# Cluster attention feeding two FFN stages: the row maxima placed by a small transfer, throwaway products, and a new sequence

## The chip, the cores and the metric

The kernel runs on one core of a Trainium2 chip. TensorE (PE) multiplies, VectorE (DVE), ScalarE (ACT) and GpSimd (POOL) work elementwise, SyncE (SP) issues most transfers. The metric is the device time of one execution in microseconds.

## What is computed

The reference, cut to what matters, with B = 2, H = 8, S = 768, D = 64, 16 clusters, 1536 tokens of 512 numbers, a hidden width of 2048, 8 experts of 4 slots:

```python
q_assign = argmax(normalized(q) @ normalized(centroids).T)   # per head, k the same
mask = q_assign[..., :, None] == k_assign[..., None, :]
scores = where(mask, q @ k.T / sqrt(D), -1e9)
attn = exp(scores - scores.max(-1)); attn /= attn.sum(-1) + 1e-9
x = (attn @ v) laid out as tokens x 512
h = x @ w_in; x = (h * clip(h + 3, 0, 6) / 6) @ w_out
logits = x @ phi                      # soft MoE: d is a softmax over tokens, c over slots
slot_in = d.T @ x; slot_out = relu(slot_in @ w1) @ w2 per expert
out = c @ slot_out
```

## The kernel before

**Heads.** The 16 heads (2 batches of 8) are numbered i. A head has 768 rows in six tiles of 128. Its queries and keys are split into high and low half-precision parts and turned by transposing transfers into two operands: `qk1t` (high and low parts) and `qk2t`, whose partitions 0 to 63 carry the high parts, 64 to 79 the one-hot cluster, and 96 to 101 rows for the maxima. For each tile n, `maxq` (L514) multiplies the first 80 partitions into a tile `sm`, and `maxr` (L530, on DVE) reduces it to one maximum per row, in column 96 + n of `mxs`. When the six columns are there, `shift` turns `mxs` on PE (L537, into a corner of the last `sm` tile) and DVE writes the result, times a diagonal, into the six rows 96 to 101 of `qk2t` (L539). `scores` (L552 with `qk1t`, L556 with 102 partitions of `qk2t`) then gives scores with mask and maximum already subtracted in tile `st`. `exps` (L600, L331 on ACT) makes probabilities, `plow` (L341 on POOL) their low parts, `pv` (L622 to L643) multiplies by v into `acc`, `finish` divides on DVE.

So the first L556 of a head needs the maxima of all six tiles: it waits for L539 of that head.

**FFN.** Every 128 tokens (12 token tiles) `xtrans` turns x by a transfer (L678), `hid` multiplies by w_in (L693), `act` applies the gate (L710, L712, L331, L341), `logits` follows, `dispatch` (L802) adds to `z`. Weights are loaded by SP and split into half-precision parts on DVE and ACT beside the heads (`narrow`, L861 to L871). The FFN of the first batch lies among heads 8 to 15, that of the second behind the last head.

**Tail.** `zsum` and `norm` (L1172, L1177, L1186), `slot_in` (`si`, L1199), `slot_t` (`sit`, L1216), `layer1` (`e`, L1324), `turn` (`ht`, L1348), `layer2` and `layer2_part` (L1361, L1381), `combine` (`po`, L1305) and the stores. Expert weights arrive in `wk` tiles through SP.

**Order.** The kernel is cut into generators (events). A string `ORDER` lists, step by step, which event goes on, and `ROOMS` fixes which buffer each tile takes:

```python
def flush():
    with tc.manual_schedule():
        for x in ORDER.split():
            next(events[int(x)], None)
```

So the order on each engine is what the string says. The queue of SP is one list too: a transfer that waits holds those behind it.

Of the kernel before, what the change touches and what calls it, by code (L numbers as in the profile page):

```python
# [8 lines left out]
F16 = mybir.dt.float16  # L9
# [8 lines left out]
P = 128  # L18
# [202 lines left out]
def clustered_attention_ffn_softmoe(ctx: ExitStack, tc, q, k, v, cent, w_in, w_out, phi, w1, w2, out):  # L221
# [76 lines left out]
    def consts():  # L298
# [6 lines left out]
        for t in qk2:  # L305
            nc.gpsimd.memset(t[:, :, :, 80:128], 0.0)
            nc.gpsimd.memset(t[:, :, 1, 96 : 96 + NT], SH)
            yield

    def consts2():  # L310
# [9 lines left out]
        for t in mxs:  # L320
            nc.gpsimd.memset(t, 0.0)
# [1133 lines left out]
```

## Time and profile before

| what | value |
|---|---|
| median of 3 runs | 486.13 us (485.87 to 487.93) |
| the profiled execution | 487.06 us, of which the span of the core's work is 485.0 us |
| busy share of the span | PE 89%, DVE 60%, ACT 65%, POOL 51% |
| mean granted clock of PE | 0.974 of full speed |

The 2.06 us between the span and the time lie around the work of the engines. The busy shares are means over stages with different limits: heads 0 to 7 with the splitting of weights (to about 135 us), heads 8 to 15 with the FFN of the first batch (to about 328 us), the FFN of the second batch (to about 420 us), and the tail.

### The profile page before, as it was taken

What the parts mean: (1) busy time and instruction counts of PE and PEld (TensorE: products, weight loads), DVE (VectorE), ACT (ScalarE), POOL (GpSimd) and SP (SyncE); (2) the same over time, 40 slices, a digit from 0 to 9 for tenths busy, and PEclk for the clock granted to TensorE, in tenths of its full rate; (3) what the DMA queues carried; (4) which work ended last, traced back from release to release, by engine and by line L of the source; (5) the groups of instructions that cost most, each with busy time, mean ns of one, the idle gap of its engine ahead of it and who ended that gap; (6) DMA issues with size and microseconds to landing.
All of it is one profiled execution on the core that took longest, in us unless ns stands there. A gap on an engine that the chain in (4) does not pass through costs nothing.

```text
span 485.0 us, 11609 instructions
## 1 busy us (share of the span) xinstructions
PE 431.3 (89%) x4802; PEld 275.4 (57%) x4802; DVE 289.4 (60%) x497; ACT 317.6 (65%) x518; POOL 249.3 (51%) x227
## 2 busy tenths in 40 slices
PE   1569899989979999999999998989998999789964
PEld 1337677768767556655656766744544455523443
DVE  4999999999978388466656868313324324421322
ACT  5759899889967679766989998953545444501121
POOL 4337686876545257656869897983133133030000
PEclk9999999999989999999999999999999999789986
DMA  7799767948690985865396533019994999999997
GB/s 226 209 164 203 194 166 202 258 145 226 189 250 18 213 206 109 190 164 106 66 246 148 109 64 66 1 20 189 295 366 95 304 268 330 381 317 351 329 268 223
DMA packets 133813, 95.48 MB, mean 197 GB/s; under 512 B 96385, under 2 KB 119425, under 8 KB 133761
## 3 DMA queue, kind: packets, MB, share of 16 engines
q1 hardware_dynamic: 129088, 88.95, 69.8%
q10 hardware_dynamic: 4672, 5.80, 3.3%
q8 instruction: 37, 0.61, 0.5%
q14 instruction: 16, 0.12, 0.1%
HBM read 64.06 MB, written 7.34 MB: 147 GB/s over the span
## 4 chain that ended last, share of the span: by engine, by line
PE 50%; DVE 17%; DMA 11%; ACT 8%; issue 4%; POOL 4%; SPq 1%; ACTq 0%; DVEq 0%; POOLq 0%
PE h L693 20%; DVE mxs L530 5%; PE sm L514 3%; PE st L552 3%; DMA qk1t<-qk 3%; PE st L556 3%; PE e L1324 3%; DMA wod<-in_moe_w_out_dram 3%; DMA wk<-in_moe_w_dram 2%; DMA qk2t<-qk 2%; ACT p L600 2%; POOL pp L341 2%; PE o L1361 2%; ACT pp L331 1%; PE z L802 1%
## 5 line engine op out<-in xcount | busy, mean ns | idle before, releaser
L341 POOL TENSOR_TENSOR pp<-p,pp 128x768 f16<-128x768 f32 x72 | 117.8, 1645 | 60.1 <-ACT pp L331 34.9
L693 PE MATMUL h<-wq,xt 128*128 128x512 f16 x576 | 131.5, 379 | 1.0 <-DMA xt<-xhl 1.0
L530 DVE TENSOR_REDUCE mxs<-sm 128x1 f32<-128x768 f32 x96 | 88.8, 951 | 15.0 <-PE sm L514 14.4
L693 PEld LDWEIGHTS <-xt 128*128 128x128 f16 x576 | 55.4, 98 | 64.0 <-issue 2.5
L341 POOL TENSOR_TENSOR ghl<-r,ghl 128x1024 f16<-128x1024 f32 (+1 forms) x25 | 50.3, 2011 | 71.3 <-ACT ghl L331 61.3
L600 ACT ACTIVATE p<-st 128x768 f32<-128x768 f32 x72 | 58.0, 809 | 9.2 <-PE st L556 7.5
L331 ACT ACTIVATE pp<-p 128x768 f16<-128x768 f32 x72 | 60.3, 843 | 1.2
L552 PE MATMUL st<-qk1t 128*128 128x384 f16 x192 | 48.2, 333 | 6.0 <-ACT p L600 2.8
L712 DVE SCALAR_TENSOR_TENSOR r<-r,h 128x1024 f32<-128x1024 f32 (+1 forms) x26 | 29.5, 1136 | 36.8 <-ACT r L710 35.4
L514 PE MATMUL sm<-qk2t 80*128 80x384 f16 x192 | 46.0, 338 | 4.1 <-DVE mxs L530 1.9
L556 PE MATMUL st<-qk2t 102*128 102x384 f16 x192 | 48.4, 333 | 0.0
L710 ACT ACTIVATE r<-h,b_relu 128x1024 f32<-128x1024 f32 (+1 forms) x26 | 27.2, 1045 | 30.9 <-PE h L693 19.2
L622 PE MATMUL acc<-v,pp 128*128 128x65 f32 x288 | 36.2, 276 | 0.2 <-DVE oh L457 0.2
L622 PEld LDWEIGHTS acc<-v,pp 128*128 128x128 f32 x288 | 35.2, 194 | 1.7 <-issue 0.5
L628 PE MATMUL acc<-v,pp 128*128 128x64 f16 x432 | 36.1, 194 | 0.0
L627 PE MATMUL acc<-v,pp 128*128 128x65 f16 x432 | 36.1, 192 | 0.0
L341 POOL TENSOR_TENSOR qk<-qk,qk 128x768 f16<-128x768 f32 x15 | 25.5, 1698 | 19.4 <-ACT qk L331 19.1
L331 ACT ACTIVATE ghl<-r 128x1024 f16<-128x1024 f32 (+1 forms) x26 | 25.6, 987 | 13.4 <-DVE r L712 11.1
L627 PEld LDWEIGHTS <-pp 128*128 128x128 f16 x432 | 31.2, 99 | 2.7
L628 PEld LDWEIGHTS <-pp 128*128 128x128 f16 x432 | 29.2, 96 | 2.7
L331 ACT ACTIVATE qk<-qk 128x768 f32<-128x768 f32 (+2 forms) x32 | 25.9, 818 | 6.0 <-DMA qk1t<-qk 4.2
L635 PE MATMUL acc<-v,pp 128*128 128x65 f16 x432 | 24.9, 194 | 2.6 <-POOL pp L341 2.6
(193 smaller groups left out, 763.5 us busy)
## 6 DMA issues: line engine op xcount, KB each, us to landing
wk<-in_moe_w_dram SPq DMA_DIRECT2D x60, 512.0 KB, 8.3
wi<-in_moe_w_in_dram SPq DMA_DIRECT2D x16, 512.0 KB, 6.3
wod<-in_moe_w_out_dram SPq DMA_DIRECT2D x16, 512.0 KB, 4.8
wos<-wo ACTq DMA_DIRECT2D x8, 512.0 KB, 3.6
wk<-wos SPq DMA_DIRECT2D x8, 512.0 KB, 5.0
qk<-in_q_dram SPq DMA_DIRECT2D x16, 192.0 KB, 3.5
qk<-in_k_dram SPq DMA_DIRECT2D x16, 192.0 KB, 3.8
v<-in_v_dram SPq DMA_DIRECT2D x16, 192.0 KB, 2.9
```

The source lines that it names most:

```text
L331: nc.scalar.activation(out, in_, AF.Copy, scale=scale)
L341: (nc.vector if e == "v" else nc.gpsimd).tensor_tensor(out=out, in0=in_, in1=hi, op=ALU.subtract)
L514: nc.tensor.matmul(s[:, j, 0:384], d["qk2t"][0:80, n, 0], d["qk2t"][0:80, 3 * j : 3 * j + 3, 1], start=True, stop=True,)
L530: nc.vector.tensor_reduce(out=mxs[i % 2][:, 96 + n : 97 + n], in_=s[:, :, 0:384], op=ALU.max, axis=AX.XY)
L552: nc.tensor.matmul(s[:, j, 0:384], d["qk1t"][:, t, 1], d["qk1t"][:, 3 * j : 3 * j + 3, 0], start=True, stop=False)
L556: nc.tensor.matmul(s[:, j, 0:384], d["qk2t"][0 : 96 + NT, t, 1], d["qk2t"][0 : 96 + NT, 3 * j : 3 * j + 3, 0], start=False, stop=True,)
L600: nc.scalar.activation(p32, s[:, :, 0:384], AF.Exp, scale=sc_exp)
L622: nc.tensor.matmul(o, p32[:, j, r * P : (r + 1) * P], d["v32"][:, t], start=(t == 0 and n == 0), stop=False)
L627: nc.tensor.matmul(o, hi, v1[:, t, 0:65], start=(t == 0 and n == 0), stop=False)
L628: nc.tensor.matmul(o[:, 0:64], hi, v1[:, t, 65:129], start=False, stop=False)
L693: nc.tensor.matmul(s[:, fb % 2], xt[:, lhs], wq[fb][:, hl, kk], start=(n == 0), stop=(n == 11))
L712: nc.vector.scalar_tensor_tensor(out=g, in0=r, scalar=6.0 * SG, in1=sf, op0=ALU.min, op1=ALU.mult)
```

## The change

The turned maxima become six rows of 128 numbers on six partitions. One DVE operation (L556 of the changed kernel) scales them into a small tile `row`, and a transfer from SP (L558) lays the 768 numbers one behind the other into a single partition (96) of `qk2t`. `mxs` shrinks to six columns, the score product reads 97 partitions in place of 102, and a constant row of the operand is one row in place of six. A function `keep` issues matmuls into a PSUM tile that nobody reads; 47 of these events (108 products) stand ahead of the turn of head 1's maxima, one (two products) among the last heads, and 13 (26 products) in the tail. `ORDER` and `ROOMS` are new.

```diff
-    mxs = [ap.tile([P, 96 + NT], F32, name=f"mxs_{i}", bufs=1) for i in range(2)]
+    mxs = [ap.tile([P, NT], F32, name=f"mxs_{i}", bufs=1) for i in range(2)]
-            nc.gpsimd.memset(t[:, :, 1, 96 : 96 + NT], SH)
+            nc.gpsimd.memset(t[:, :, 1, 96:97], SH)
-        for t in mxs:
-            nc.gpsimd.memset(t, 0.0)
+    def keep(n, m):
+        t = pss(f"kw_{n}")
+        for _ in range(m):
+            nc.tensor.matmul(t[:, 0, 0:256], ident16, ident.bitcast(F16), start=True, stop=True)
+        yield
-            d["mt"] = s[0 : 96 + NT, 0, 384:512]
+            d["mt"] = s[0:NT, 0, 384:512]
-        nc.vector.tensor_reduce(out=mxs[i % 2][:, 96 + n : 97 + n], in_=s[:, :, 0:384], op=ALU.max, axis=AX.XY)
+        nc.vector.tensor_reduce(out=mxs[i % 2][:, n : n + 1], in_=s[:, :, 0:384], op=ALU.max, axis=AX.XY)
         nc.tensor.transpose(pm, mxs[i % 2], ident)
         yield
-        nc.vector.scalar_tensor_tensor(
-            out=d["qk2t"][96 : 96 + NT, :, 0],
-            in0=pm[96 : 96 + NT].unsqueeze(1).to_broadcast([NT, NT, P]),
-            scalar=-(2.0**29),
-            in1=nident[96 : 96 + NT, 96 : 96 + NT].unsqueeze(2).to_broadcast([NT, NT, P]),
-            op0=ALU.max,
-            op1=ALU.mult,
-        )
+        row = sm.tile([NT, P], F16, tag="row", name=f"row_{i}", bufs=2)
+        nc.vector.tensor_scalar(out=row, in0=pm, scalar1=-1.0 / SH, scalar2=2.0**29 / SH, op0=ALU.mult, op1=ALU.min)
+        yield
+        nc.sync.dma_start(out=d["qk2t"][96:97, :, 0], in_=row)
-                d["qk2t"][0 : 96 + NT, t, 1],
-                d["qk2t"][0 : 96 + NT, 3 * j : 3 * j + 3, 0],
+                d["qk2t"][0:97, t, 1],
+                d["qk2t"][0:97, 3 * j : 3 * j + 3, 0],
+    for n in range(7):
+        ev(keep, n, 4)
+    for n in range(40):
+        ev(keep, 7 + n, 2)
+    for n in range(14):
+        ev(keep, 47 + n, 2)
```

Head 8 on DVE, before. The rows are the last reductions of its maxima (`mxs`), the division of head 7 (`den`, `xa`), and the write of the six rows (L539):

```order
L530 TENSOR_REDUCE mxs_113<-sm_3_2346 128x1
L652 TENSOR_SCALAR den_2383<-acc_2231 128x6
L653 RECIPROCAL den_2383<-den_2383 128x6
L655 TENSOR_TENSOR xa_2386<-acc_2231,den_2383 128x384
L530 TENSOR_REDUCE mxs_113<-sm_0_2388 128x1
L440 TENSOR_TENSOR as_2295<-as_2295,ac_2408 128x12x16
L539 SCALAR_TENSOR_TENSOR qk2t_2290<-sm_5_2326,nident 6x6x128
L443 TENSOR_REDUCE mx_2452<-as_2295 128x12
```

The same place on DVE in the changed program:

```order
L546 TENSOR_REDUCE mxs_113<-sm_5_2490 128x1
L546 TENSOR_REDUCE mxs_113<-sm_0_2510 128x1
L664 TENSOR_SCALAR den_2547<-acc_2407 128x6
L665 RECIPROCAL den_2547<-den_2547 128x6
L667 TENSOR_TENSOR xa_2550<-acc_2407,den_2547 128x384
L556 TENSOR_SCALAR row_2569<-sm_5_2490 6x128
L456 TENSOR_TENSOR as_2577<-as_2577,ac_2608 128x12x16
L459 TENSOR_REDUCE mx_2634<-as_2577 128x12
```

The write into `qk2t` is now the scaling into `row`, still behind the division of head 7; one cluster operation (`as`) that stood ahead of it stands behind it.

On SP at the same time, before: the turned operand of head 8 (`qk2t`), v, and two transposes of x for the FFN (`xt`):

```order
L476 DMA_TRANSPOSE qk2t_2290<-qk_2_106 128x12x128
L356 DMA v_2411<-in_v_dram 128x384
L678 DMA_TRANSPOSE xt_2480<-xhl_732 128x8x128 x2
L352 DMA qk_2573<-in_q_dram 128x384
L352 DMA qk_2573<-in_k_dram 128x384
L905 DMA wod_0_2578<-in_moe_w_out_dram 128x1024 x2
```

And now, from the same transpose of `qk2t` on:

```order
L492 DMA_TRANSPOSE qk2t_2431<-qk_2_106 128x12x128
L372 DMA v_2439<-in_v_dram 128x384
L420 DMA_TRANSPOSE qk1t_2506<-qk_9_1978 128x12x128
L558 DMA qk2t_2431<-row_2569 1x6x128
L690 DMA_TRANSPOSE xt_2637<-xhl_900 128x8x128
L917 DMA wod_0_2717<-in_moe_w_out_dram 128x1024 x2
```

Behind that transpose of `qk2t` stand v, the transpose of the next head's `qk1t` (new at this place), and then the new transfer of `row`; the transpose of x comes behind it.

On PE at the end of the second FFN, before: the last product of the dispatch (`z`), a turned tile (`pe`), and the sums of `zsum` (`zt`):

```order
L802 LDWEIGHTS dhl_6412
L802 MATMUL z_6417<-ghl_6094,dhl_6412 32x512
L788 MATMUL pe_6441<-ident,et_6435 128x128
L1172 MATMUL zt<-nident,zacc 128x128 x4
L1177 LDWEIGHTS ghl_6220
```

And now:

```order
L814 LDWEIGHTS dhl_6601
L814 MATMUL z_6610<-ghl_6273,dhl_6601 32x512
L360 LDWEIGHTS ident_86
L360 MATMUL kw_6624<-ident,ident_86 128x256
L360 LDWEIGHTS ident_86
L360 MATMUL kw_6624<-ident,ident_86 128x256
L800 MATMUL pe_6635<-ident,et_6627 128x128
L1188 MATMUL zt<-nident,zacc 128x128 x4
L1193 LDWEIGHTS ghl_6425
```

Two throwaway products (`kw`) stand between the dispatch and the turned tile. Others stand behind `si`, around `ht` and among `po`.

## Rows read from the trace of the kernel before

**Rows 1.** By stage: length, busy PE, PEld, DVE, ACT, POOL (instructions), clock, DMA share, GB/s.

```profile
0.00:25.00 25.00, 9.36 (x80) 6.29 (x80) 17.31 (x36) 16.31 (x28) 10.58 (x50) 1.00 0.77 220
25.00:135.00 110.00, 100.44 (x1173) 78.10 (x1173) 104.47 (x160) 95.08 (x145) 73.19 (x51) 1.00 0.75 193
135.00:206.00 71.00, 67.25 (x729) 44.70 (x726) 47.39 (x78) 52.76 (x81) 38.17 (x26) 0.98 0.72 164
206.00:296.00 90.00, 89.38 (x1134) 56.65 (x1131) 59.26 (x106) 76.12 (x130) 70.05 (x45) 1.00 0.62 130
296.00:328.00 32.00, 28.21 (x422) 18.67 (x418) 12.21 (x26) 23.80 (x36) 26.44 (x19) 1.00 0.06 12
328.00:420.00 92.00, 85.08 (x726) 45.02 (x725) 32.73 (x59) 45.05 (x85) 26.84 (x14) 0.99 0.93 275
420.00:485.00 65.00, 51.58 (x557) 25.95 (x557) 16.05 (x36) 8.44 (x19) 4.05 (x26) 0.84 0.94 303
```

**Rows 2.** Waits on DVE from 25 to 135 us: waiter, releaser, microseconds, times, longest.

```profile
DVE mxs L530 <- PE sm L514: 1.0, 3, 0.5
```

**Rows 3.** Groups on DVE, shapes apart: busy us, mean ns, idle before.

```profile
L530 DVE TENSOR_REDUCE mxs<-sm 128x1 f32<-128x768 f32 x96 | 88.8, 951 | 15.0 <-PE sm L514 14.4
...
L539 DVE SCALAR_TENSOR_TENSOR qk2t<-sm,nident 6x768 f16<-6x768 f32 x16 | 15.4, 964 | 4.5 <-PE sm L537 4.2
...
L498 DVE TENSOR_SCALAR mv<-cm,emp 16x65 f16<-16x65 f32 x16 | 4.6, 287 | 0.5
...
L494 DVE TENSOR_SCALAR emp<-cm 16x1 f32<-16x1 f32 x16 | 2.5, 156 | 6.8 <-PE cm L491 6.4
```

**Rows 4.** Timeline of head 8's turn: start, duration, engine, line.

```profile
156.79 0.32 PE L537 MATMUL sm<-ident,mxs 128*102 128x128 f32 x1
...
157.14 0.96 DVE L539 SCALAR_TENSOR_TENSOR qk2t<-sm,nident 6x768 f16<-6x768 f32 x1 [0.36 <-PE sm L537]
...
158.63 0.49 PE L552 MATMUL st<-qk1t 128*128 128x384 f16 x2
...
158.95 0.49 PE L556 MATMUL st<-qk2t 102*128 102x384 f16 x2
```

**Rows 5.** Transfers: times issued, KB, median us from issue to landing.

```profile
qk2t<-qk SPq DMA_TRANSPOSE x15, 4.8
...
c<-in_centroids_dram ACTq DMA_DIRECT2D x1, 32.0 KB, 2.8
```

**Rows 6.** Issue times on SP in its timeline, a plain transfer.

```profile
0.73 0.41 SPq L352 DMA_DIRECT2D qk<-in_q_dram  x1
```

**Rows 7.** The same from 136 to 162 us, two transposes.

```profile
157.22 3.42 SPq L678 DMA_TRANSPOSE xt<-xhl  x2
```

**Rows 8.** Waits on SP, whole program.

```profile
SPq L721 <- POOL ghl L341: 12.7, 3, 8.3
```

**Rows 9.** PE groups from 18 to 32 us.

```profile
L514 PE MATMUL sm<-qk2t 80*128 80x384 f16 x12 | 4.2, 512 | 0.5 <-DVE qk2t L385 0.5
```

**Rows 10.** PE groups from 50 to 125 us.

```profile
L514 PE MATMUL sm<-qk2t 80*128 80x384 f16 x58 | 13.2, 325 | 2.0 <-DVE mxs L530 1.2 <-DMA qk2t<-qk 0.6
```

**Rows 11.** Busy time by stage in the tail, columns as in rows 1.

```profile
418.00:429.00 11.00, 9.13 (x90) 4.74 (x94) 3.77 (x12) 1.85 (x7) 0.00 (x0) 0.53 0.93 350
429.00:447.00 18.00, 16.73 (x155) 5.57 (x148) 2.19 (x4) 0.76 (x2) 4.05 (x26) 1.00 0.98 341
```

**Rows 12.** The chain that ended last, from 400 us: start, us, what.

```profile
419.75 4.38 DMA wk<-in_moe_w_dram
...
424.90 5.63 PE si L1199 x32
...
432.83 13.94 PE e L1324 x128
...
458.15 7.28 DMA wk<-in_moe_w_dram
...
473.52 3.42 PE o L1381 x64
```

334 rows, old and new, of tables (ORDER, ROOMS) are left out of this document.

## Prediction

> **What bounds the kernel now.** I read the busy times by stage first, since the shares over the whole span mix stages with different limits. From 25 to 135 us DVE works 104.47 of 110 us and PE 100.44 [rows 1]: both are nearly full, and the view of waits says which of them leads. In this stretch DVE waited for PE's product of the maxima three times, 1.0 us in all [rows 2]. DVE therefore sets the pace of heads 0 to 7, and PE, with 9.6 us idle, follows. From 135 to 206 us PE works 67.25 of 71 us and DVE 47.39; from 206 to 296 PE works 89.38 of 90 and DVE 59.26. There DVE has time to spare. From 296 to 328 us ACT (23.80 of 32) and POOL (26.44) take turns with PE, and the DMA share is 0.06. Behind 328 PE works 92% of its time with a DMA share of 0.93, and in the tail it is a chain of products, small DVE steps and weight transfers, at a clock of 0.84 [all rows 1].
>
> So a microsecond taken from DVE before 135 us is worth most of a microsecond: all that follows is PE work that starts as much earlier. The second batch's transfers start after the 0.06 stretch, so the weight stream moves with it. The same microsecond taken behind 135 us is worth nothing.
>
> **The DVE write.** The old write into six rows takes 964 ns, sixteen times [rows 3]. The new one goes over 6 by 128 numbers. The nearest row is a scaling over 16x65, 287 ns; one over 16x1 takes 156 ns [rows 3]. I take 0.29 us, since 128 numbers for each partition are nearer to 65 than to 1; the ends are 0.156 and the old 0.964. It saves 0.964 − 0.29 = 0.67 us for each head. Seven writes, of heads 0 to 6, lie ahead of the last maxima of head 7 on DVE, and the eighth of head 7 right behind: 7 to 8 x 0.67 = 4.7 to 5.4 us. I take **−5.0** (ends 0 and 8 x 0.81 = −6.5). The other eight writes are in stages where DVE waits anyway: 0.
>
> **The transfer of the row.** No row of before shows a transfer from partitions to one partition. The nearest is the smallest plain load, 32 KB, 2.8 us from issue to landing; the turned operand, on the same queue under load, takes 4.8 [rows 5], and issuing a plain transfer takes 0.41 us on SP [rows 6], the least that it can cost. I take 2.8, since the row is small like the first. Sixteen issues are 16 x 0.41 = 6.6 us of SP, which is idle far longer than this.
>
> The path from the turn to the first product that reads the row was 0.32 of PE and 0.96 of DVE; head 8 shows 2.16 us between them (156.79 to 158.95), filled by other products [rows 4]. It is now 0.32 + 0.29 + 2.8 = 3.4 us. The new sequence puts more work in between: for head 8 the same two kinds of weight products as before, and twelve cluster products and a group of weight products besides, so somewhat over 2.2 us; PE would then lack up to 1.2 us. By the changed order heads 3, 4, 5, 9, 10 and 12 have the products of a whole probability tile there and lack nothing. Of the ten others, 0, 1, 2, 6 and 7 lie in the stage in which PE has 9.6 us to spare [rows 1] and DVE has maxima of the next head to do. That leaves 8, 11, 13, 14 and 15, where PE is the bound: at 0.4 us each, about a third of the 1.2, **+2.0** (ends 0, and at 4.8 us for a transfer 5 x 3.2 = +16, which is the slower rival below).
>
> The Trainium skill, page "DMA: Bandwidth & Descriptors", section on the anatomy of one DMA, says that a transfer has a fixed cost of about 2.0 us, nearly all of it the confirmation at the end, however few bytes it moves. That speaks against this change: each head's path gets a 2 us piece for a DVE saving of 0.67. By that figure the path would be 0.32 + 0.29 + 2.0 = 2.6 us, and the five heads would lack about 0.4 us at most, near the sum that I took. No run shows so small a transfer yet.
>
> **Throwaway products at the start.** 108 products of 256 columns: two of 384 columns take 0.32 us from one line's start to the next [rows 4], so one takes 0.107 us at full clock, and 108 take 11.5 us, twice that at half. PE has 25 − 9.36 = 15.6 us idle in the first 25 us [rows 1] and waits for casts and transfers there, so I count them at nothing; if they stood in front of ready products they would cost up to 11.5 us. They may raise the clock: the product of the maxima takes 512 ns from 18 to 32 us [rows 9] and 325 ns later [rows 10], though the clock column shows 1.00 for both. Since DVE is busy 17.31 of the first 25 us, and its reductions of 0.95 us are longer than the two products that feed each, a faster PE shortens only the first heads' lead-in: **−0.5** (0 to −1.5). With it goes the smaller setting of constants on POOL, in the same lead-in.
>
> **Throwaway products in the tail.** From 418 to 429 us the granted clock is 0.53, from 429 to 447 it is 1.00 [rows 11]. The 32 products of `si` take 5.63 us there, where 128 of `e` at full clock take 13.94, that is 0.109 each [rows 12]: 32 x 0.109 = 3.5, so the low clock costs 2.1 us at `si`. The last 64 products of L1381 take 3.42 us [rows 12], at half clock again by that comparison if they cost half of 0.107 at full. But two products of 256 columns are 0.2 to 0.4 us, against a wait of 4.38 us for a transfer right ahead of `si` [rows 12]; I expect the level to stay low at most of these places. **−0.5** for the clock (0 to −4), **+0.5** for 26 products on the path (26 x 0.107 = 2.8 if none were hidden).
>
> **The sequence** itself moves work between heads; the work ahead of the last maxima of head 7 is the same in kind and number but for the writes. I count it at nothing, ±1.
>
> **Sum.** −5.0 + 2.0 − 0.5 − 0.5 + 0.5 = −3.5 us, from the profiled execution's 487.06: 483.6. That execution lies 0.93 us above the median of 486.13, so against the median **482.6 us**.
>
> **The rivals.** *Gain eaten* (no change, 485 to 487): the rows arrive late in the five heads where PE bounds, at 1.0 us each in place of 0.4, and PE, already at 91% from 25 to 135 us [rows 1], takes 2 us of the gain there as soon as DVE gives way. −3.5 + 3.0 + 2.0 = +1.5 at the worst, 484 to 487.5. For it speaks that PE is so near DVE in that stage; against it, DVE's waits of only 1.0 us.
>
> *Rows held in the queue* (slower, about 491): SP is one list. The row of head 8 stands right behind a transpose, and two transposes take 3.42 us to issue [rows 7]; the rows of heads 9 to 12 stand behind transposes of the gated hidden tiles, and those waited for POOL up to 8.3 us, 12.7 us in three waits [rows 8], 4.2 each. If four rows are late by 2 us beyond their cover and the five heads lack 0.4 still, PE loses 8 us where it is full: 482.6 + 8 = 490.6. It decides from about 1.5 us for each of these four heads (6 us) on. Against it: the maxima of a head come about when its transposes are through, and three waits are few.
>
> *Clock held* (faster than I say, about 479): if the products at both ends keep the clock at its higher level, the start gives 1 us more, `si` 2.1 and L1381 1.0 more: 482.6 − 0.5 − 3 = 479. The Trainium skill, page "TensorE: Matmul & The Clock Gate", part 1, says that the throttled state is the default and that activity releases it, which would be the reason for these products; what it would do here is this rival. The trace agrees in that `si`, behind idle time, runs at 0.53 and `e`, behind 5.6 us of `si`, at 1.00.
>
> **How the numbers follow.** About 0.5% (2.4 us) is what a measurement of this kernel can tell from no change: below 483.7 is faster, above 488.6 slower. My forecast has 0.45, of which 0.42 lies below 483.7 (480.5 to 483.7 is its core); clock held 0.20, all of it faster; gain eaten 0.18, the same; rows held 0.17, slower. That makes faster 0.62, same 0.21, slower 0.17. The range from 477 to 488.5 leaves out the rival of the queue (0.17 at most) and a little below.
>
> **What would show it.** Right: the new DVE operation at about 0.29 us; DVE's busy time down by about 10.7 us (16 x 0.67); the last maxima of head 7 reduced 4 to 6 us earlier than before; from there to the end a gain that shrinks by less than 2 us; PE waiting for the row transfer at a few heads, under 1 us each; `si` still near 5.6 us. Wrong: row transfers of 4 us and more, or rows whose issue stands behind a waiting transpose, with PE idle ahead of L568 in the stretch up to 300 us; or a DVE that becomes idle before 135 us, with PE the bound, so that less than half of the 5 us arrives; or `si` at 3.5 us, which would put the time lower than I say.

## The result

Over 20 executions each, the changed kernel takes 482.21 us in the median and the kernel before 488.12. The ratio is 0.9866, with a 95% interval from 0.9821 to 0.9911: faster, by 1.3%. The ratios here leave out the executions that took over 1.5% more than the fastest of their kernel, while the medians take all of them, so the two can differ by up to one per cent (0.9898 by the ratio, 0.9797 by the medians, for one kernel below). The forecast was 482.6 us and faster. The number held; two of its main terms did not.

The profiled execution of the changed kernel took 485.73 us, in the upper part of its runs; a second one, taken with the experiments, took 484.4. Both show the same picture up to 135 us. Stages of the changed kernel, columns as in [rows 1]:

```profile
0.00:25.00 25.00, 18.93 (x177) 13.70 (x177) 17.55 (x37) 15.42 (x27) 10.52 (x48) 1.00 0.87 234
25.00:135.00 110.00, 100.29 (x1100) 76.74 (x1097) 90.92 (x151) 90.03 (x138) 66.02 (x46) 0.91 0.69 181
...
206.00:296.00 90.00, 88.99 (x1093) 55.59 (x1090) 55.16 (x105) 75.76 (x131) 68.71 (x44) 1.00 0.65 119
...
420.00:483.90 63.90, 51.97 (x596) 25.80 (x596) 16.75 (x38) 9.41 (x22) 4.09 (x26) 0.94 0.98 322
```

PE is busy 18.93 us of the first 25, where it was 9.36: the throwaway products. From 25 to 135 us DVE works 90.92 us in place of 104.47, but PE is no further ahead, and its clock is 0.91. Only part of that difference is saved work: eight shorter writes make 8 x 0.69 = 5.5 us, and DVE ran 151 operations there in place of 160. DVE's groups with shapes apart:

```profile
L546 DVE TENSOR_REDUCE mxs<-sm 128x1 f32<-128x768 f32 x96 | 88.3, 952 | 22.0 <-PE sm L530 21.4
...
L556 DVE TENSOR_SCALAR row<-sm 6x128 f16<-6x128 f32 x16 | 4.4, 275 | 4.0 <-PE sm L553 3.9
```

The new operation takes 275 ns where 290 were forecast, and the whole line 4.4 us where it was 15.4 [rows 3]. So DVE did get its 11 us, over all sixteen heads. The timeline shows what became of them. SP first:

```profile
53.26 0.73 SPq L558 DMA_DIRECT2D qk2t<-row  x1
54.04 0.43 SPq L368 DMA_DIRECT2D qk<-in_q_dram  x1
54.53 1.48 SPq L368 DMA_DIRECT2D qk<-in_k_dram  x1
56.05 0.91 SPq L892 DMA_DIRECT2D wi<-in_moe_w_in_dram  x2
```

Then DVE:

```profile
58.37 1.22 DVE L883 SCALAR_TENSOR_TENSOR wi<-wi,nt_i 128x1024 uint32<-128x1024 uint32 x1
62.66 1.29 DVE L873 TENSOR_SCALAR nw_i<-wi 128x1024 uint32<-128x1024 uint32 x1 [3.06 <-DMA wi<-in_moe_w_in_dram]
63.87 0.94 DVE L546 TENSOR_REDUCE mxs<-sm 128x1 f32<-128x768 f32 x1
```

And PE:

```profile
61.05 0.49 PE L568 MATMUL st<-qk2t 97*128 97x384 f16 x2
64.86 0.80 PE L530 MATMUL sm<-qk2t 80*128 80x384 f16 x2 [3.32 <-DVE mxs L546]
```

The row of head 2 leaves at 53.26 us. Behind it on SP stand two loads of queries and keys and the weight load `wi`, which leaves at 56.05. DVE waits 3.06 us for it, until 62.66, PE waits 3.32 us for DVE, until 64.86, and within PE's wait, at 62.7, its clock falls. The same place by stage:

```profile
60.00:68.00 8.00, 4.68 (x42) 2.89 (x40) 4.47 (x8) 4.08 (x8) 3.42 (x3) 0.67 0.70 165
68.00:72.00 4.00, 4.00 (x25) 2.75 (x24) 2.64 (x7) 3.37 (x5) 3.19 (x2) 0.50 0.20 56
72.00:76.00 4.00, 4.00 (x32) 3.49 (x32) 3.87 (x6) 1.76 (x2) 2.19 (x2) 0.50 0.58 207
76.00:80.00 4.00, 4.00 (x47) 3.74 (x47) 1.67 (x2) 3.70 (x5) 0.33 (x1) 0.96 0.85 164
```

From 68 to 76 us the granted clock is 0.50, 1.2 GHz. It falls while PE is idle and comes back when PE has been busy throughout both stretches. Waits on SP that ended with a row, and PE's waits for a row, in the changed kernel:

```profile
SPq L558 <- DVE row L556: 28.6, 8, 10.1
```

```profile
PE st L568 <- DMA qk2t<-row: 1.3, 1, 1.3
```

SP waited 28.6 us for rows, up to 10.1 at once. All its waits at a row's transfer, whichever operation the profile names as their end, come to 53.5 us; while SP waits there, it issues nothing else. PE waited for a row's transfer once, 1.3 us. So the first suspect is what stands behind a row on SP, and not the row itself; the experiments test it.

### The profile page after: what moved, and what is told of

The parts are those of the page before. It is cut to its first block, busy times and chain, and to the rows that moved or that the text cites. A ratio compares the mean times of both kernels' runs of the same rounds, so it can differ in the third digit from the quotient of the medians.

```text
span 483.9 us, 11910 instructions
## 1 busy us (share of the span) xinstructions
PE 444.6 (92%) x4938; PEld 285.6 (59%) x4938; DVE 273.0 (56%) x497; ACT 317.3 (66%) x518; POOL 247.4 (51%) x225
## 4 chain that ended last, share of the span: by engine, by line
PE 48%; DMA 8%; ACT 5%; DVE 5%; POOL 3%; issue 2%; SPq 1%; POOLq 0%; DVEq 0%; ACTq 0%
PE h L705 23%; PE e L1340 3%; DMA wk<-in_moe_w_dram 3%; POOL pp L351 2%; PE sm L530 2%; DMA wod<-in_moe_w_out_dram 2%; DMA qk2t<-qk 2%; PE st L564 2%; PE st L568 2%; ACT p L612 2%; ACT pp L341 2%; PE o L1397 1%; PE z L814 1%; PE acc L647 1%; SPq L1036 1%
## 5 line engine op out<-in xcount | busy, mean ns | idle before, releaser
L568 PE MATMUL st<-qk2t 97*128 97x384 f16 x192 | 48.6, 335 | 1.4 <-DMA qk2t<-row 1.3
L634 PEld LDWEIGHTS acc<-v,pp 128*128 128x128 f32 x288 | 36.7, 200 | 1.3 <-PE sm L530 0.2
L639 PE MATMUL acc<-v,pp 128*128 128x65 f16 x432 | 36.7, 194 | 0.0
L639 PEld LDWEIGHTS <-pp 128*128 128x128 f16 x432 | 32.3, 101 | 2.9 <-issue 0.4
L640 PEld LDWEIGHTS <-pp 128*128 128x128 f16 x432 | 29.8, 97 | 2.3
L530 PEld LDWEIGHTS <-qk2t 80*128 80x128 f16 x192 | 17.4, 102 | 22.3 <-issue 10.6
```

Of the source, the lines that this page charges most:

```text
L530: nc.tensor.matmul(s[:, j, 0:384], d["qk2t"][0:80, n, 0], d["qk2t"][0:80, 3 * j : 3 * j + 3, 1], start=True, stop=True,)
L568: nc.tensor.matmul(s[:, j, 0:384], d["qk2t"][0:97, t, 1], d["qk2t"][0:97, 3 * j : 3 * j + 3, 0], start=False, stop=True,)
L634: nc.tensor.matmul(o, p32[:, j, r * P : (r + 1) * P], d["v32"][:, t], start=(t == 0 and n == 0), stop=False)
L639: nc.tensor.matmul(o, hi, v1[:, t, 0:65], start=(t == 0 and n == 0), stop=False)
L640: nc.tensor.matmul(o[:, 0:64], hi, v1[:, t, 65:129], start=False, stop=False)
```

## The experiments

In the table, "products" are the throwaway products; medians are in microseconds, over 6 or 12 executions each, beside that of the kernel before, measured with them ("together" below).

| kernel | median | before | ratio (95% interval) |
|---|---|---|---|
| new sequence alone | 487.64 | 487.61 | 1.0035 (0.9996 to 1.0074) |
| sequence, row transfer | 487.19 | 487.61 | 1.0034 (0.9981 to 1.0087) |
| changed, no products at the start | 486.27 | 487.61 | 0.9979 (0.9931 to 1.0026) |
| before, row transfer | 553.38 | 487.61 | 1.1325 (1.1251 to 1.1398) |
| changed, again | 481.40 | 487.92 | 0.9939 (0.9896 to 0.9981) |
| changed, old write | 478.35 | 487.92 | 0.9812 (0.9725 to 0.9898) |
| changed, no products in the tail | 485.78 | 487.92 | 0.9914 (0.9863 to 0.9965) |
| changed, rows from ACT's queue | 508.95 | 487.92 | 1.0456 (1.0383 to 1.0528) |
| old write, idle transfers | 485.36 | 489.60 | 0.9960 (0.9910 to 1.0010) |
| changed, short write, no transfer | 475.85 | 489.60 | 0.9796 (0.9724 to 0.9868) |
| changed, old write, again | 479.68 | 489.60 | 0.9898 (0.9829 to 0.9968) |
| before, products at the start | 503.24 | 489.60 | 1.0364 (1.0304 to 1.0424) |

**The new sequence alone.** The write into six rows is put back, and `keep` issues nothing. The main lines of the edit (the wider `mxs`, the constant rows and the 102 partitions come back too):

```diff
-        for _ in range(m):
+        for _ in range(0):
             nc.tensor.matmul(t[:, 0, 0:256], ident16, ident.bitcast(F16), start=True, stop=True)
-        row = sm.tile([NT, P], F16, tag="row", name=f"row_{i}", bufs=2)
-        nc.vector.tensor_scalar(out=row, in0=pm, scalar1=-1.0 / SH, scalar2=2.0**29 / SH, op0=ALU.mult, op1=ALU.min)
-        yield
-        nc.sync.dma_start(out=d["qk2t"][96:97, :, 0], in_=row)
+        nc.vector.scalar_tensor_tensor(out=d["qk2t"][96 : 96 + NT, :, 0], ...)
+        yield
```

> The new sequence alone: the maxima are written into six rows by DVE as before, and no throwaway product is issued (the events stay, empty). Theory A (the shorter DVE write is the gain): nothing gained, ratio to before 0.995 to 1.005. Theory B (the throwaway products at the start are the gain, because PE's clock is up from 4.6 us in place of 32.9): the same, 0.995 to 1.005, with the first granted clock record back near 30 us. Theory C (the sequence is the gain): 0.985 to 0.992.

The median is that of before: the sequence by itself is worth nothing. In its profiled execution one stretch stands out; columns as in [rows 1]:

```profile
41.00:56.00 15.00, 13.89 (x117) 11.54 (x117) 8.83 (x12) 7.35 (x12) 9.97 (x6) 0.54 0.55 136
```

PE is busy 13.89 of 15 us at a clock of 0.54 there, and DVE works only 8.83 and waits for PE's products of the maxima:

```profile
DVE mxs L548 <- PE sm L532: 6.0, 2, 5.1
```

Ahead of it PE waits for the long write of head 1 (0.96 us on DVE):

```profile
42.11 1.44 PE L532 MATMUL sm<-qk2t 80*128 80x384 f16 x4 [1.22 <-DVE qk2t L557]
```

Theory C falls. Whether the clock falls there in each execution is not known from one profile.

**Sequence and row transfer, no products.** Only the first of the two edits above.

> The changed kernel without any throwaway product (the events stay, empty). Theory A: it keeps the gain, ratio 0.985 to 0.992. Theory B: no gain or a loss, 0.996 to 1.005, since the start is slow again and the rows only add waits. Theory C: 0.985 to 0.992.

487.19: the shorter write with its transfers is worth nothing either, so the gain is not there without the products. Theory A falls as it stood: the 11 us of DVE bring nothing with the transfers beside them. This kernel has no products either, and yet its clock stays up where that of the sequence alone fell; at the same place PE waits 0.45 us for the short operation:

```profile
41.00:56.00 15.00, 14.97 (x198) 12.21 (x196) 13.61 (x23) 13.30 (x21) 12.67 (x9) 1.00 0.57 130
```

```profile
40.74 0.81 PE L530 MATMUL sm<-qk2t 80*128 80x384 f16 x4 [0.45 <-DVE row L556]
```

So the low clock from 41 to 56 us does not come from the lack of products alone.

**No products at the start.**

```diff
-        for _ in range(m):
+        for _ in range(m if n >= 47 else 0):
```

> The changed kernel without the 108 throwaway products at the start, with those of the tail. Theory A: as the changed kernel, 0.985 to 0.990. Theory B: the last maximum of head 0 comes about 4 us later than in the changed kernel (26 to 27 us in place of 22.8), and 3 to 4 us are lost at the end: 0.993 to 1.000. If DVE hides the start, the 4 us have gone by head 7.

486.27, within 0.5% of before, against 482.21 and 481.40 with them. The 108 products, from which I had expected 0.5 us, are needed for most of the gain. The profiles do not show where they bring it: from 41 to 56 us the clock is 1.00 here too, and the last maximum of head 7 starts at 134.40 us here and at 136.13 without any products, against 139.06 and 136.90 in the two profiles of the changed kernel. The four profiled executions hardly differ in time (483.06, 485.73, 485.73 and 484.36 us), and this one was the fastest of its twelve.

**The kernel before with the row transfer**, in its own sequence; the transfer is issued directly behind the scaling.

> The kernel before, in its own sequence, with the maxima scaled into a row and laid down by the transfer (issued right behind the scaling, wherever that stood). Theory A: DVE saves 0.67 us a head and the transfers cost little: 0.990 to 0.995. Theory B: the rows arrive late in a sequence that was not laid out for them and the gain on DVE is eaten: 0.998 to 1.015, with PE waiting for the rows at several heads.

65.8 us slower, far beyond what either theory gave. Waits on SP:

```profile
SPq L539 <- DVE row L538: 77.2, 11, 16.2
SPq L539 <- DVE as L442: 26.4, 2, 16.4
```

Waits on PE:

```profile
PE sm L512 <- DMA qk2t<-qk: 18.6, 5, 6.0
PE lg L738 <- DMA gt<-ghl: 10.0, 5, 4.3
```

In these two lines SP waited 103.6 us for the rows and for an operation ahead of them, up to 16.4 at once; all its waits at a row's transfer come to 131 us, against 53.5 in the changed kernel. The transposes behind them came late: PE waited 18.6 us for `qk2t` and 10.0 for the turned hidden tiles. This is the rival of the rows held in the queue, at eight times its price, in a sequence that was not laid out for it.

**The changed kernel again.**

> The changed kernel as it is, on the chip of the other runs of this call, for their sake: ratio 0.983 to 0.991 by all theories. The profile is a second look at it: I expect the stretch from 62.7 to 76.3 us at the lower clock, behind a wait of DVE for a weight load, to be there again if it belongs to the sequence (a load held on SP behind a row), and to be absent if it was chance.

481.40, and the wait for `wi` is there again, so it was not chance. DVE from 25 to 135 us:

```profile
DVE mxs L546 <- PE sm L530: 6.2, 8, 2.2
DVE nw_i L873 <- DMA wi<-in_moe_w_in_dram: 3.3, 1, 3.3
```

**The changed kernel with the old write**, products and sequence kept (the second edit above alone).

> The changed kernel, throwaway products and all, with the maxima written into six rows by DVE as before and no transfer. If the shorter DVE write is part of the gain once the start is fast (theory A, in part): 0.992 to 1.000, since DVE has 16 x 0.69 = 11 us more to do. If the gain is the throwaway products' alone (theory B): as the changed kernel or better, 0.980 to 0.990.

478.35, and 479.68 when it was measured again: 3.05 us under the changed kernel, measured together, with 16 x 0.69 = 11 us more for DVE. SP and DVE at the place where the changed kernel waited:

```profile
51.13 0.43 SPq L370 DMA_DIRECT2D qk<-in_q_dram  x1
51.61 0.43 SPq L370 DMA_DIRECT2D qk<-in_k_dram  x1
52.14 0.85 SPq L899 DMA_DIRECT2D wi<-in_moe_w_in_dram  x2
```

```profile
59.67 1.23 DVE L890 SCALAR_TENSOR_TENSOR wi<-wi,nt_i 128x1024 uint32<-128x1024 uint32 x1
60.81 0.69 DVE L880 TENSOR_SCALAR nw_i<-wi 128x1024 uint32<-128x1024 uint32 x1
```

The load `wi` leaves at 52.14 in place of 56, and DVE takes it up without a wait. Over the stage DVE is busy 102.65 of 110 us and PE's clock is 0.98; in the stretch that was at 0.54 with the sequence alone it is 1.00:

```profile
25.00:135.00 110.00, 102.77 (x1211) 80.61 (x1211) 102.65 (x162) 98.40 (x148) 72.80 (x50) 0.98 0.75 195
```

```profile
41.00:56.00 15.00, 14.77 (x186) 12.09 (x182) 13.70 (x22) 13.19 (x19) 12.49 (x11) 1.00 0.68 152
```

**No products in the tail.**

```diff
-        for _ in range(m):
+        for _ in range(m if n < 47 else 0):
```

> The changed kernel without its last 28 throwaway products. Without those at the start the median was 486.27, without any 487.19; so those of the tail are worth about 0.9 us and this should come to about 483 (ratio 0.988 to 0.993), with the products of si in the tail at half clock again (5.6 us in place of about 4). If they are worth nothing: 0.983 to 0.989 and si as in the changed kernel.

Median and ratio disagree: 4.4 us more than the changed kernel by the medians, measured together, nothing by the ratios (0.9914 against 0.9939, intervals overlapping). `si` stays at 595 ns for each of its 32 products (861 before), as in the changed kernel; and it is so even in the profile of the sequence alone. So `si` at full clock came with the new sequence, not with the products next to it. What the 28 products of the tail are worth stays open.

**Rows from ACT's queue.**

```diff
-        nc.sync.dma_start(out=d["qk2t"][96:97, :, 0], in_=row)
+        nc.scalar.dma_start(out=d["qk2t"][96:97, :, 0], in_=row)
```

> The changed kernel with the 16 row transfers issued from ACT's queue, so that no row's wait holds loads on SP. If the row's place on SP costs (SP waited 28.6 us for rows, at most 10.1): 1 to 4 us faster than the changed kernel, 0.977 to 0.985. If that wait costs nothing: 0.984 to 0.995, ACT paying up to 16 x 0.7 = 11 us of issue, part of it on the path.

Worse by 27.6 us than the changed kernel. On ACT the issue stands in line with ACT's own work (the first row leaves 2.3 us after its scaling began, from SP 0.8), and now PE does wait for the rows:

```profile
PE st L568 <- DMA qk2t<-row: 22.2, 9, 5.5
```

**Idle transfers.** Old write and products; at each place of a row transfer on SP, one of the same size that nobody reads.

```diff
         yield
+        row = sm.tile([NT, P], F16, tag="row", name=f"row_{i}", bufs=2)
+        nc.sync.dma_start(out=row, in_=d["qk2t"][96 : 96 + NT, 0, 0])
```

> The changed kernel with throwaway products and the old write into six rows, and besides at each place of a row transfer on SP a transfer of the same size out of the written rows into a tile that nobody reads. PE and DVE never wait for it; SP waits for the write as it did for the row. If the row's loss is the queue (loads held on SP behind the wait): the 478 us of the old write without transfers go back to 481 to 486 (ratio 0.987 to 0.997), with the late weight load and the low clock near 63 to 72 us. If the loss is PE's waiting for the rows themselves: 477 to 480, as without the transfers.

485.36 against 479.68 without them, measured together: 5.7 us by the medians for transfers whose data nobody uses, 3.0 us of 488 by the ratios, from 0.9898 to 0.9960 (the intervals overlap; medians and profiles point the same way). DVE's waits for loads are back, and the last maximum of head 7 starts at 134.06 us in place of 129.86, or 130.56 in the second profile of the old write (the lines stand below):

```profile
DVE nw_i L882 <- DMA wi<-in_moe_w_in_dram: 2.9, 2, 2.3
DVE nw_o L882 <- DMA wod<-in_moe_w_out_dram: 2.0, 1, 2.0
```

So a large part of the rows' loss comes with nobody waiting for a row. It is their place on SP: the wait (62.3 us at these transfers) and the issue (0.72 us for one) together, which this run does not separate. In the changed kernel the same maximum comes another 3 to 5 us later, although its DVE operation is shorter, so the idle transfers do not make up the whole loss.

**Short write, no transfer.** DVE writes one piece of 6 by 128 straight into the operand; five sixths of the subtraction are left out.

```diff
-        nc.vector.scalar_tensor_tensor(out=d["qk2t"][96 : 96 + NT, :, 0], ...)
+        nc.vector.tensor_scalar(
+            out=d["qk2t"][96 : 96 + NT, 0, 0], in0=pm[96 : 96 + NT], scalar1=-1.0 / SH, scalar2=2.0**29 / SH,
+            op0=ALU.mult, op1=ALU.min,
+        )
```

> The changed kernel with throwaway products and no transfer, DVE writing only one of the six row pieces straight into the operand (6 by 128; five sixths of the subtraction of the maxima are left out). It shows what the shorter DVE operation is worth if nothing comes with it. If DVE bounds the first eight heads, as the prediction says: 3 to 5 us under the old write, 473 to 475 (ratio 0.970 to 0.976). If PE is so near that the cut is absorbed: 476 to 479.

475.85 against 479.68, measured together: 3.8 us by the medians, 0.0102 by the ratios, which is 5.0 us of 488, with intervals that overlap. This is what the shorter DVE operation is worth with nothing behind it. A wait for `wi` is here too, with no transfer ahead of it on SP, since DVE comes to it sooner:

```profile
DVE nw_i L876 <- DMA wi<-in_moe_w_in_dram: 2.0, 1, 2.0
```

PE waited 2.28 us for DVE behind it, and the clock stayed at 1.00 from 25 to 135 us. So not the whole of the changed kernel's 3.06 us is the queue's. The last maximum of head 7 starts at 126.69 us, with the old write at 129.86, in the changed kernel at 136.90:

```profile
126.69 0.95 DVE L548 TENSOR_REDUCE mxs<-sm 128x1 f32<-128x768 f32 x1
```

```profile
129.86 0.95 DVE L548 TENSOR_REDUCE mxs<-sm 128x1 f32<-128x768 f32 x1
```

```profile
136.90 0.95 DVE L546 TENSOR_REDUCE mxs<-sm 128x1 f32<-128x768 f32 x1
```

With the old write and idle transfers:

```profile
134.06 0.95 DVE L548 TENSOR_REDUCE mxs<-sm 128x1 f32<-128x768 f32 x1
```

**The old write again**, beside the last two.

> The changed kernel with throwaway products and the old write, beside the other kernels of this call: 476 to 481 (ratio 0.976 to 0.986). If the first look's six runs were lucky, as the changed kernel: 481 to 483.

479.68, ratio 0.9898 (0.9829 to 0.9968). Sequence and products with the old write beat the kernel before both times; against the changed kernel their medians, 9.6 and 9.9 us under before, stand against 5.9 and 6.5, but the intervals of the ratios overlap (0.9898 and 0.9812 against 0.9866 and 0.9939).

**The kernel before with products at the start**, 92 of them, placed by me in PE's waits:

```diff
+                for n, m in KW.get(key + (done[key],), ()):
+                    t = pss(f"kw_{n}")
+                    for _ in range(m):
+                        nc.tensor.matmul(t[:, 0, 0:256], ident16, ident.bitcast(F16), start=True, stop=True)
                 next(events[int(x)], None)
```

> The kernel before in its own sequence, with 92 throwaway products of 256 columns in the waits of PE in the first 30 us. If the products alone are the gain: PE's first granted clock record moves from 32.9 to about 5 us, the last maximum of head 0 from 26.9 to 23 to 25 us, and the end 2 to 4 us earlier (ratio 0.990 to 0.996). If it takes the new sequence to use them: 0.997 to 1.003.

13.6 us slower, and no test of the question: my products waited themselves and held the real products behind them. That the PSUM tiles which I gave them were still being read is my reading; the profile names only the DVE operation with which the wait ended:

```profile
PE kw L278 <- DVE wi L885: 9.3, 2, 5.7
```

It shows only that a throwaway product in a wrong place or buffer can cost more than it gives.

## Why the prediction was right in the number and wrong in its steps

**DVE bounds heads 0 to 7: right, as far as the clock stays up.** The view of waits said so, and the short write without a transfer brought 3.8 us by medians and 5.0 by the ratios (the intervals overlap), where −5.0 stood in the sum. The 0.29 us for the operation was 0.275.

**The row transfer: the term that failed.** The sum had +2.0, for rows that come late in the five later heads where PE is the bound. PE waited for a row once, 1.3 us in one profiled execution and 1.5 in the other, at head 7. The cost is about 7 us (the changed kernel stands 6.5 us under before, the short write without transfers 13.7; by the ratios 0.9939 against 0.9796), and the idle transfers give 5.7 of it by the medians and 3.0 by the ratios; what the rest is was not tried alone. Most of it lies in the first eight heads, where the last maximum of head 7 comes 10.2 us later than with the short write, and where I had put the path of the row at nothing because PE had idle time: I asked who waits for the row, and not what waits behind it on SP. SP's issue took 0.73 us for a row, not 0.41. The rival of the held queue had the mechanism, but with the wrong place (heads 8 to 12) and the wrong victim (the rows themselves, where it was the weight loads and what follows them). With it the whole DVE gain was eaten: sequence and row without products measure as before. The last maximum of head 7, which I expected 4 to 6 us earlier, came 3.3 us later in the second profiled execution (136.90) and 5.5 in the first (139.06). Before, and with the sequence alone:

```profile
133.57 0.95 DVE L530 TENSOR_REDUCE mxs<-sm 128x1 f32<-128x768 f32 x1
```

```profile
139.67 0.95 DVE L548 TENSOR_REDUCE mxs<-sm 128x1 f32<-128x768 f32 x1
```

The work ahead of this mark is nearly the same in all of them: 1236 products on PE before, 1217 in the changed kernel besides the thrown-away ones, 192 and 193 operations on DVE. So by the profiles the changed kernel is behind at head 7 and gains later: from the mark to the end of the span it takes 345.6 and 344.8 us, the kernel before 351.4, the sequence alone 347.9. This is the reverse of the forecast, which had the gain ahead of the mark and a loss of up to 2 us behind it. `si`, below, is 2 us of it.

The 2.8 us for a transfer lie between what was measured. At head 7 of the second profiled execution the row left SP at 138.80 us, and PE, which waited for it, read it at 143.36, 4.56 us later, in a stretch with a DMA share of 0.94:

```profile
138.80 0.73 SPq L558 DMA_DIRECT2D qk2t<-row  x1
```

```profile
143.36 0.80 PE L568 MATMUL st<-qk2t 97*128 97x384 f16 x2 [1.48 <-DMA qk2t<-row]
```

At head 15, with a DMA share of 0.01, 1.74 us passed from the issue to the product that reads the row:

```profile
308.71 0.68 SPq L558 DMA_DIRECT2D qk2t<-row  x1
```

```profile
310.45 0.48 PE L568 MATMUL st<-qk2t 97*128 97x384 f16 x2
```

The fixed cost of about 2.0 us in the Trainium skill (page "DMA: Bandwidth & Descriptors", section on the anatomy of one DMA) is given there for transfers that GpSimd issues, which the prediction left out. This transfer, issued by SP, took at most 1.74 us where the transfer engines were idle, and 4.56 where they were busy.

**The products at the start: the second term that failed, the other way.** I counted them at −0.5. With the old write, sequence and products stand 9.6 and 9.9 us under before, where the sequence alone stands at 0.0; with the rows it is 6.5 against 0.4. The changed kernel without them measures 486.27. In the profiles of the old write with and without products, the last maximum of head 7 starts at 129.86 with them and at 139.67 without. Part of it is the lead-in. PE's products of head 0's maxima, from 12 to 24 us, with the old write, without and with products:

```profile
L532 PE MATMUL sm<-qk2t 80*128 80x384 f16 x12 | 4.7, 509 | 2.0 <-DVE qk2t L403 1.5 <-DVE mxs L548 0.5
```

```profile
L532 PE MATMUL sm<-qk2t 80*128 80x384 f16 x12 | 2.9, 324 | 0.8 <-DVE qk2t L403 0.6 <-DVE mxs L548 0.2
```

They are faster with them (324 ns against 509); the clock column shows 1.00 for both, so on this stretch it tells nothing. The larger part, by these two profiles, is the stretch from 41 to 56 us shown above: at 0.54 without products, at 1.00 with them. DVE is the bound of this stage and I had argued that a faster PE cannot help; but DVE waited 6.0 us for PE in that stretch. At the lower clock it is PE that sets the pace. This explains the old write alone: with the short operation the clock there is 1.00 without products too, and still they are worth 4.9 us by the medians (486.27 against 481.40). For the changed kernel it stays open how they do it. A hint is the granted clock over all executions, whose median is 0.979 in the second measurement of the changed kernel, 0.972 without the products at the start and 0.967 without any. The run that put products into the old sequence doesn't tell.

**The products in the tail** were forecast at −0.5 and +0.5 and stay open. `si` went from 5.63 to 3.67 us, as the rival of the held clock said, but the sequence did that without them.

**The sum.** By medians: 0 for the sequence, about −10 for the products, −3.8 for the shorter write, and about +7 for the rows: −6 to −7, against −3.5 forecast. The split depends on the order in which the parts are put in: with the rows in place the products are worth 5.8 (487.19 against 481.40), not 10. Two errors of opposite sign, about −9 and +5, partly hid each other, and the median of before, 486.13 from three runs, was 488.12 from twenty. Three of the prediction's own signs of being wrong did show: DVE idle before 135 us (90.92 of 110 busy), a row that took over 4 us, and `si` near 3.5. That the number held was luck, and no proof of the reasons.

## What to carry to other kernels

A transfer that replaces work on a busy engine has to be priced twice: by who needs its data, and by what stands behind it in the queue that issues it, since its wait holds loads that have nothing to do with it. Measure the two apart with a transfer of the same place and size that nobody reads. Where an engine's clock follows its work, a short stall in one stage can cost more than its length (here PE's wait of 3.32 us stood at the start of 13.6 us at the lower clock in one profile, 6.8 in the other), so a bound read from busy shares holds only as long as the clock stays up.

## What the runs showed of the hardware

The 20 executions of the changed kernel go from 474.21 us at a mean granted clock of 0.994 to 488.23 at 0.964, with one program. Within one profile some falls to 0.5 come inside a long wait of PE (62.7 us, in a wait of 3.32 us), others behind shorter ones (at about 41.7 us in the run of the sequence alone, in a wait of 1.22 us, with PE busy 9.29 of the 11 us up to 41). A wait of 2.28 us in the short write (until 62.51 us) was followed by none, one of 2.46 with the idle transfers (until 65.24) by one. The two profiles of the changed kernel agree on the first fall (62.7 and 64.4 us, in the same wait) and not on all the later ones.
